# A fused attention and two-layer-block kernel: row sums on VectorE in the first softmaxes, another order of sums in a weight pair, and alternating first token tiles

## The chip, the cores and the metric

The kernel runs on one core of a Trainium2 chip. The metric is device time in microseconds (us) of one execution. TensorE (PE) multiplies matrices into PSUM banks, ScalarE (ACT) and VectorE (DVE) read PSUM and SBUF, GpSimd (POOL) works on SBUF alone, SyncE (SP) issues all DMA transfers. Each engine works through its own instructions in the order in which they were written down; an instruction that waits holds up everything behind it on its engine.

## What is computed

Three stages follow each other, all in float32 with 2304 tokens of 512 channels:

```
# attention in chunks of 64 tokens, 4 batches x 8 heads, head width 64
scores = q_c @ k_c.T / 8
attn = exp(scores - max(scores)); attn = attn / (sum(attn) + 1e-9)
x = (attn @ v_c) laid out as (2304, 512)
# mixture of 4 experts, F = 1024
p = probs / (probs.sum(-1) + 1e-9)
x = sum over e of p[:, e] * (relu(x @ w1[e]) @ w2[e])
# normalised gated block, F = 1536
xn = x / sqrt(mean(x*x) + 1e-6) * rms_g
g, val = xn @ w_gate, xn @ w_val
out = (g * sigmoid(g) * val) @ w_out
```

## The kernel before, in words

**Number format.** Each float32 operand of a matmul is split into two pieces of a shorter format, a high one (`hh`, `[:, 0]`) and a low one (`hl`, `[:, 1]`), and a product is three matmuls (line 22). The low piece is always one subtraction that waits for the copy that makes the high piece.

**Tokens.** The 18 tiles of 128 tokens go through in three sets of six. A set has two halves of three tiles (index b = 0 or 1, 384 tokens). After attention come the expert stage of all three sets ("moe", eight blocks of work per set) and then the gated stage of all three ("glu", three blocks per set), 33 blocks in all.

**One block** consists of `hidden` for two pairs of hidden columns (in glu for gate and value of each), and then `outer`. `hidden` (line 751) computes four products, for b = 0, 1 and j = 0, 1 (two groups of 128 hidden columns), by seven products of sums of quarters of x and w instead of eight. Each of the seven is six matmuls of 384 columns (`product`, line 701). VectorE combines them: partial sums u2, u3 and five additions per pair, reading PSUM banks named a, b, c and d. A finished combination goes to `use`, which makes hh on ScalarE and leaves the making of hl (and the return of the bank) in a list that `catch_up` empties later. The combinations are finished in the order (1,1), (0,0), (1,0), (0,1).

**`outer`** (line 846) multiplies hh and hl with the second weights for tile t = 0 to 5; tiles 0 to 2 belong to b = 0, tiles 3 to 5 to b = 1. A tile takes 12 matmuls of 512 columns: six of the block's first pair, then six of its second. VectorE adds the result to an accumulator (`flush`). Of its second six, the first tile needs (0,0) and then (0,1) of the pair that `hidden` has only just left.

**Order of the work.** The program is written out in full by Python generators. `Chains.tick`, called after each product and each six matmuls of `outer`, drops a few instructions of side work into the engines' queues: weight splitting (`operands`, ScalarE and GpSimd), decoding of 64-bit weights (VectorE), attention of the next set. `ORDER` (line 27) is the order in which the seven weight parts are made, fetched and summed.

**The start.** Attention of the first six tiles (`attention_unit` with `first_softmax`, line 612) and the first products are interleaved by `Chains.race`, which gives each engine the step that it thinks can begin first, by guessed costs such as `{"ACT": 0.9}`. When TensorE would idle by its guess, `idle` (line 957) fills in transposes into `scratch`. In `first_softmax` the exponentials are eight activations of 128x64 per tile, each with `accum_out`, so that ScalarE gives the row sums. Then VectorE inverts them and GpSimd scales.

Names in the rows: `sc` scores, `e` exponentials, `at` scaled attention, `trA`/`aT` its transpose, `pv` attention times v, `x` split x, `w` a weight or a split weight part, `r` a fetched raw weight, `o` output bank of `outer`.

Of the kernel before, what the change touches and what calls it, by code (L numbers as in the profile page):

```python
# [23 lines left out]

ORDER = (0, 5, 4, 6, 1, 3, 2)


class Slots:  # L30
# [41 lines left out]
class Chains:  # L72
# [6 lines left out]
    def add(self, gen, every=0.0, first=False, busy=None):  # L79

        c = [gen, every, self.clock, every if busy is None else busy]
        self.chains.insert(0, c) if first else self.chains.append(c)
        return c
# [67 lines left out]
def fused_kernel(ctx, tc, qkv, probs, w12, wglu, gvec, out):  # L151
# [460 lines left out]
    def first_softmax(sc, ex, att):  # L612

        mx, nb, rs = (sm.tile([P, 2, HP], F32, tag=f"f{n}", name=n) for n in ("mx", "nb", "rs"))
        for h2 in range(2):
            nc.vector.tensor_reduce(
                mx[:, h2, :].unsqueeze(2), sc[h2][:, :HP * CH].rearrange("p (g n) -> p g n", n=CH), axis=AX.X, op=ALU.max
            )
            yield {"DVE": 0.45 if h2 == 0 else 0.2}, 1
        nc.vector.tensor_scalar(nb, mx, -SCALE, None, op0=ALU.mult)  # L620
        for h2 in range(2):
            yield {"ACT": 0.9}, 1
            for g in range(HP):
                cols = slice(g * CH, (g + 1) * CH)
                nc.scalar.activation(  # L625
                    ex[h2][:, cols], sc[h2][:, cols], AF.Exp, scale=SCALE, bias=nb[:, h2, g:g + 1],
                    accum_out=rs[:, h2, g:g + 1],
                )
            banks.put(sc[h2])
        yield {"DVE": 0.5}, 1  # L630
        nc.vector.tensor_scalar_add(rs, rs, 1e-9)
        nc.vector.reciprocal(rs, rs)
        for h2, e in enumerate(ex):
            yield {"POOL": 0.65}, 1
            nc.gpsimd.tensor_tensor(
                att.rearrange("p (hp r n) -> p hp r n", hp=HP, r=2)[:, :, h2, :],
                e[:, :HP * CH].rearrange("p (g n) -> p g n", n=CH),
                rs[:, h2, :].unsqueeze(2).to_broadcast([P, HP, CH]),
                op=ALU.mult,
            )  # L640
            tp.put(e)
# [74 lines left out]
    def catch_up():  # L716
        while later:
            later.pop(0)()

    def bank(name):  # L720
        if not banks.free():
            work.force(None, banks.free)
        return banks.get(name)
# [27 lines left out]
    def hidden(key, use):  # L751


        w = lambda n: weight((*key, n))
        v = lambda t: t[:, :NB]
        a = bank("a_ps")
        product(a, w(0), 0, True, False)
        p1 = cp.get("p1")
        nc.scalar.copy(p1, v(a))  # L759
        catch_up()  # L760
        b = bank("b_ps")
        product(b, w(5), 5, True, True)
        u2 = cp.get("u2")
        add(nc.vector, u2, v(b), p1)
        banks.put(b)
        cp.put(p1)
        d = bank("d_ps")
        product(d, w(4), 4, True, False)
        c = bank("c_ps")
        product(c, w(6), 6, True, True)  # L770
        u3 = cp.get("u3")
        add(nc.vector, u3, v(c), u2)
        add(nc.vector, v(c), v(d), u3)
        use(1, 1, c)
        product(a, w(1), 1, False, True)
        catch_up()
        use(0, 0, a)
        c = bank("c_ps")
        product(c, w(3), 3, True, True)
        add(nc.vector, v(c), v(c), u3)  # L780
        cp.put(u3)
        catch_up()
        use(1, 0, c)
        product(d, w(2), 2, False, True)
        add(nc.vector, v(d), v(d), u2)
        cp.put(u2)
        catch_up()
        use(0, 1, d)

    hs = {}  # L790

# [54 lines left out]
    def outer(fps, w2, flush, aside):  # L846

        catch_up()
        for t in range(TPS):
            b, r = divmod(t, TPB)  # L850
            ps = bank(f"o_{t}")
            last = (len(fps) - 1, 1, len(PASSES) - 1)
            for k, fp in enumerate(fps):
                for j in range(2):
                    for m, (hx, wi) in enumerate(PASSES):
                        nc.tensor.matmul(  # L856
                            ps, hs[fp, b, j][hx][:, r * P:(r + 1) * P], w2[2 * k + j][:, wi],
                            start=((k, j, m) == (0, 0, 0)), stop=((k, j, m) == last),
                        )
                if k == len(fps) - 1:  # L860
                    flush(t, ps)
                    banks.put(ps)
                work.tick(6 * 0.227)
                aside(t * UF + k)
        for fp in fps:
            for b in range(2):
                for j in range(2):
                    hi, lo = hs.pop((fp, b, j))
                    hh.put(hi)
                    hl.put(lo)  # L870
        w2p.put(*w2)
# [53 lines left out]
    with tc.manual_schedule():  # L925
        units = [[i, i + 1] for i in range(0, NTILE, 2)]
        own = lambda s: units[s * TPS // 2:(s + 1) * TPS // 2]
        make_identity(nc, ident)
        fetching = work.add(fetch())
        lead = [[i] for i in range(TPS)]  # L930
        tiles = [attention_tiles(u) for u in lead]
# [201 lines left out]
```

## Time and profile before

| | us |
|---|---|
| median of 3 runs (1246.80 to 1248.53) | 1246.94 |
| the profiled execution | 1249.17 |
| its span | 1247.4 |
| granted TensorE clock, mean over the span | 0.997 |
| PE busy | 1223.3 (98%) |
| DVE busy | 783.0 (63%) |
| POOL busy | 537.4 (43%) |
| ACT busy | 449.0 (36%) |

The profiled execution lies 1.8 us above its span and 2.2 us above the median of the timed runs. A busy PE is not PE at its peak: matmuls overlap in the record, so time that TensorE loses shows best as the distance between the starts of two matmuls, compared with the usual distance. A clock of 1.00 is 2.4 GHz, 0.50 is 1.2 GHz.

### The profile page before, as it was taken

What the parts mean: (1) busy time and instruction counts of PE and PEld (TensorE: products, weight loads), DVE (VectorE), ACT (ScalarE), POOL (GpSimd) and SP (SyncE); (2) the same over time, 40 slices, a digit from 0 to 9 for tenths busy, and PEclk for the clock granted to TensorE, in tenths of its full rate; (3) what the DMA queues carried; (4) which work ended last, traced back from release to release, by engine and by line L of the source; (5) the groups of instructions that cost most, each with busy time, mean ns of one, the idle gap of its engine ahead of it and who ended that gap; (6) DMA issues with size and microseconds to landing.
All of it is one profiled execution on the core that took longest, in us unless ns stands there. A gap on an engine that the chain in (4) does not pass through costs nothing.

```text
span 1247.4 us, 20675 instructions
## 1 busy us (share of the span) xinstructions
PE 1223.3 (98%) x7253; PEld 1107.0 (89%) x7253; DVE 783.0 (63%) x1388; ACT 449.0 (36%) x1109; POOL 537.4 (43%) x575
## 2 busy tenths in 40 slices
PE   7999999999999999999999999999999999999998
PEld 6888899989997987889999999998998998998997
DVE  3765444456776787677677766786766634763644
ACT  7454333334243233333244224333435341332211
POOL 3696666654463563526355445354313101130100
PEclk9999999999999999999999999999999999999999
DMA  8377455554577697755667677657956935855843
GB/s 293 106 255 284 173 194 186 187 202 157 191 253 250 235 326 262 243 169 207 224 235 269 201 243 252 201 164 259 311 194 233 304 112 197 285 189 186 302 131 124
DMA packets 140215, 274.05 MB, mean 220 GB/s; under 512 B 16208, under 2 KB 16208, under 8 KB 140112
## 3 DMA queue, kind: packets, MB, share of 16 engines
q1 hardware_dynamic: 140112, 272.73, 64.0%
q8 instruction: 58, 0.95, 0.3%
q14 instruction: 45, 0.37, 0.1%
HBM read 210.28 MB, written 62.39 MB: 219 GB/s over the span
## 4 chain that ended last, share of the span: by engine, by line
PE 77%; DVE 8%; POOL 5%; issue 4%; ACT 3%; DMA 2%; SPq 0%; POOLq 0%; DVEq 0%
PE o L856 36%; PE d_ps L706 11%; PE a_ps L706 11%; PE c_ps L706 11%; PE b_ps L706 6%; POOL w L197 3%; DMA w1m<-w 2%; DVE silu L830 2%; POOL tw L197 1%; DVE c_ps L198 1%; PE pv L544 1%; DVE u L198 1%; ACT e L625 1%; PE xT L911 1%; PE sc L497 1%
## 5 line engine op out<-in xcount | busy, mean ns | idle before, releaser
L856 PE MATMUL o<-w,hh 128*128 128x512 f32 x1584 | 492.8, 392 | 5.3 <-ACT hh L796 3.5
L856 PEld LDWEIGHTS o<-w,hh 128*128 128x128 f32 x1584 | 295.7, 188 | 69.4 <-ACT hh L796 5.2
L856 PE MATMUL o<-w,hl 128*128 128x512 f32 x792 | 311.5, 393 | 2.2 <-DVE hl L799 1.2
L197 POOL TENSOR_TENSOR w<-r,w 128x512 fp32r<-128x512 f32 (+1 forms) x146 | 163.4, 1127 | 135.5 <-ACT w L356 76.7
L706 PE MATMUL c_ps<-x,w 128*128 128x384 f32 x1080 | 216.2, 336 | 0.3 <-ACT e L625 0.3
L706 PE MATMUL d_ps<-x,w 128*128 128x384 f32 x984 | 198.6, 336 | 2.4 <-DVE c_ps L198 2.2
L706 PE MATMUL a_ps<-x,w 128*128 128x384 f32 x984 | 198.6, 336 | 0.9 <-ACT p L759 0.9
L706 PEld LDWEIGHTS c_ps<-x,w 128*128 128x128 f32 x1080 | 188.8, 188 | 0.8 <-ACT e L625 0.5
L856 PEld LDWEIGHTS o<-w,hl 128*128 128x128 f32 x792 | 148.9, 188 | 39.2 <-DVE hl L197 4.7
L1049 DVE SCALAR_TENSOR_TENSOR acc<-o,pr,acc 128x512 f32<-128x512 f32 x126 | 94.3, 749 | 135.0 <-PE o L856 134.7
L197 POOL TENSOR_TENSOR hl<-silu,hh 128x384 fp32r<-128x384 f32 x54 | 54.4, 1030 | 288.4 <-ACT hh L833 288.3
L706 PEld LDWEIGHTS a_ps<-x,w 128*128 128x128 f32 x984 | 173.4, 188 | 3.9 <-ACT p L759 1.2
L706 PEld LDWEIGHTS d_ps<-x,w 128*128 128x128 f32 x984 | 172.1, 188 | 4.4 <-DVE c_ps L198 4.3
L198 POOL TENSOR_TENSOR w<-w,sc 128x512 f32<-128x512 f32 x36 | 47.1, 1309 | 163.0 <-DVE sc L415 139.8
L197 POOL TENSOR_TENSOR w<-tw,w 128x256 fp32r<-128x256 f32 x112 | 87.2, 787 | 39.9 <-ACT w L231 34.2
L198 DVE TENSOR_TENSOR u<-b_ps,p 128x384 f32<-128x384 f32 x82 | 45.5, 554 | 88.2 <-PE b_ps L706 46.4
L706 PE MATMUL b_ps<-x,w 128*128 128x384 f32 x492 | 99.0, 335 | 0.0
L759 ACT COPY p<-a_ps 128x384 f32<-128x384 f32 x82 | 39.5, 482 | 162.4 <-PE a_ps L706 162.3
L796 ACT ACTIVATE hh<-c_ps 128x384 fp32r<-128x384 f32 x100 | 49.1, 494 | 131.9 <-DVE c_ps L198 130.3
L198 DVE TENSOR_TENSOR u<-c_ps,u 128x384 f32<-128x384 f32 x82 | 45.6, 556 | 74.1 <-PE c_ps L706 73.5
L231 ACT CAST w<-tw 128x256 fp32r<-128x256 f32 x112 | 42.6, 406 | 136.0 <-POOL tw L197 91.4
L706 PEld LDWEIGHTS b_ps<-x,w 128*128 128x128 f32 x492 | 86.4, 188 | 0.1
(109 smaller groups left out, 1346.5 us busy)
## 6 DMA issues: line engine op xcount, KB each, us to landing
w<-wgv SPq DMA_DIRECT2D x252, 256.0 KB, 3.9
w<-w1m SPq DMA_DIRECT2D x224, 256.0 KB, 5.2
r<-in_w SPq DMA_DIRECT2D x128, 256.0 KB, 4.8
w1m<-w SPq DMA_DIRECT2D x112, 256.0 KB, 2.5
wgv<-w SPq DMA_DIRECT2D x84, 256.0 KB, 4.7
raw<-in_wglu SPq DMA_DIRECT2D x36, 512.0 KB, 3.8
w<-wou SPq DMA_DIRECT2D x36, 512.0 KB, 7.4
wou<-q SPq DMA_DIRECT2D x24, 256.0 KB, 4.4
```

What stands on the lines that cost most here:

```text
L197: sub = lambda eng, o, a, b: eng.tensor_tensor(o, a, b, op=ALU.subtract)
L198: add = lambda eng, o, a, b: eng.tensor_tensor(o, a, b, op=ALU.add)
L231: nc.scalar.copy(halves(out[n])[:, 0], at[part_of[n]])
L497: nc.tensor.matmul(sc[h2][c * CH:(c + 1) * CH, n:n + CH], q, k, start=True, stop=True)
L544: nc.tensor.matmul(ps[n][lo:lo + CH, o:o + CH], vt[a][lo:lo + CH, hp, ch, :], aT[a][lo:lo + CH, q:q + CH], start=True, stop=True,)
L625: nc.scalar.activation(ex[h2][:, cols], sc[h2][:, cols], AF.Exp, scale=SCALE, bias=nb[:, h2, g:g + 1], accum_out=rs[:, h2, g:g + 1],)
L706: nc.tensor.matmul(ps[:, :NB], wv[:, wi, k, :], xs[n][:, xi, k, :], start=(first and k == 0 and m == 0), stop=(last and k == KH - 1 and m ...
L759: nc.scalar.copy(p1, v(a))
L796: nc.scalar.activation(hi, src, AF.Relu)
L830: nc.vector.tensor_tensor(v, ps[:, :NB], v, op=ALU.mult)
L856: nc.tensor.matmul(ps, hs[fp, b, j][hx][:, r * P:(r + 1) * P], w2[2 * k + j][:, wi], start=((k, j, m) == (0, 0, 0)), stop=((k, j, m) == last),
L1049: nc.vector.scalar_tensor_tensor(out=acc[i], in0=ps, scalar=pr[:, i, e:e + 1], in1=acc[i], op0=ALU.mult, op1=ALU.add,)
```

## The change

Four edits. (1) At the start a tiny activation of type Exp on a zeroed column is put ahead of everything. (2) In `first_softmax` the activations lose `accum_out`; two VectorE reductions per tile, one for each half, make the row sums. The costs that `race` is told change, and with them the order of the start. (3) In `hidden` the banks c and d change roles: v4 = d + u2 is made while product 6 runs, then d = c + v4 ends (1,1); bank c goes on accumulating in place of d; the order of finishing is (1,1), (0,0), (0,1), (1,0), and `ORDER` follows. (4) In `outer` the first four groups of six matmuls go tile 0 pair 1, tile 1 pair 1, tile 0 pair 2, tile 1 pair 2, with two output banks open.

```diff
-ORDER = (0, 5, 4, 6, 1, 3, 2)
+ORDER = (0, 5, 4, 6, 1, 2, 3)
...
-                    ex[h2][:, cols], sc[h2][:, cols], AF.Exp, scale=SCALE, bias=nb[:, h2, g:g + 1],
-                    accum_out=rs[:, h2, g:g + 1],
+                    ex[h2][:, cols], sc[h2][:, cols], AF.Exp, scale=SCALE, bias=nb[:, h2, g:g + 1]
                 )
             banks.put(sc[h2])
-        yield {"DVE": 0.5}, 1
+        for h2 in range(2):
+            yield {"DVE": 0.4 if h2 == 0 else 0.8}, 2 - h2
+            nc.vector.tensor_reduce(
+                rs[:, h2, :].unsqueeze(2), ex[h2][:, :HP * CH].rearrange("p (g n) -> p g n", n=CH), axis=AX.X, op=ALU.add
+            )
         nc.vector.tensor_scalar_add(rs, rs, 1e-9)
...
         d = bank("d_ps")
-        product(d, w(4), 4, True, False)
+        product(d, w(4), 4, True, True)
+        v4 = cp.get("v4")
+        add(nc.vector, v4, v(d), u2)
         c = bank("c_ps")
-        product(c, w(6), 6, True, True)
-        u3 = cp.get("u3")
-        add(nc.vector, u3, v(c), u2)
-        add(nc.vector, v(c), v(d), u3)
-        use(1, 1, c)
+        product(c, w(6), 6, True, False)
+        add(nc.vector, v(d), v(c), v4)
+        use(1, 1, d)
         product(a, w(1), 1, False, True)
         catch_up()
         use(0, 0, a)
-        c = bank("c_ps")
-        product(c, w(3), 3, True, True)
-        add(nc.vector, v(c), v(c), u3)
-        cp.put(u3)
+        d = bank("d_ps")
+        product(d, w(2), 2, True, True)
+        add(nc.vector, v(d), v(d), v4)
+        cp.put(v4)
+        catch_up()
+        use(0, 1, d)
+        product(c, w(3), 3, False, True)
+        add(nc.vector, v(c), v(c), u2)
+        cp.put(u2)
         catch_up()
         use(1, 0, c)
-        product(d, w(2), 2, False, True)
-        add(nc.vector, v(d), v(d), u2)
-        cp.put(u2)
-        catch_up()
-        use(0, 1, d)
...
-        for t in range(TPS):
+        last = (len(fps) - 1, 1, len(PASSES) - 1)
+        order = [(t, k) for t in range(TPS) for k in range(len(fps))]
+        order[1], order[2] = order[2], order[1]
+        open_banks = {}
+        for n, (t, k) in enumerate(order):
             b, r = divmod(t, TPB)
-            ps = bank(f"o_{t}")
...
+            if k == 0:
+                open_banks[t] = bank(f"o_{t}")
+            ps = open_banks[t]
...
+        warm = sm.tile([P, 1], F32, tag="warm", name="warm")
+        nc.vector.memset(warm, 0.0)
+        nc.scalar.activation(warm, warm, AF.Exp)
```

ScalarE's queue at the start of the program, before: the exponentials of three tiles stand one behind the other.

```order
L625 ACT_TABLE_LOAD
L625 ACTIVATE e_213,rs<-sc_195,nb 128x64 x4
L625 ACTIVATE e_214,rs<-sc_196,nb 128x64 x4
L625 ACTIVATE e_249,rs<-sc_226,nb 128x64 x4
L625 ACTIVATE e_250,rs<-sc_227,nb 128x64 x4
L625 ACTIVATE e_290,rs<-sc_263,nb 128x64 x4
L526 COPY aT_323<-trA_318 128x512
L625 ACTIVATE e_291,rs<-sc_264,nb 128x64 x4
L315 CAST w_0_360<-r_0_165 128x256
```

The same place now:

```order
L938 ACT_TABLE_LOAD
L938 ACTIVATE warm<-warm 128x1
L625 ACTIVATE e_216<-sc_198,nb 128x64 x4
L625 ACTIVATE e_217<-sc_199,nb 128x64 x4
L315 CAST w_0_289<-r_0_168 128x256
L625 ACTIVATE e_252<-sc_229,nb 128x64 x4
L625 ACTIVATE e_253<-sc_230,nb 128x64 x4
L625 ACTIVATE e_293<-sc_266,nb 128x64 x4
L526 COPY aT_333<-trA_328 128x512
L625 ACTIVATE e_294<-sc_267,nb 128x64 x4
```

The table load stands alone in front, and the split of the first fetched weight (`w_0<-r_0`) has moved from behind the third tile's exponentials to behind the first tile's; on GpSimd the subtraction that belongs to it has moved likewise ahead of the first tile's scaling.

VectorE's queue in the last value pair of the program, before (lines 198: the sums of `hidden`; 830: silu times value; 197: the low piece of (0,1)):

```order
L198 TENSOR_TENSOR u_13685<-b_ps,p_13675 128x384
L198 TENSOR_TENSOR u_13701<-c_ps,u_13685 128x384
L198 TENSOR_TENSOR c_ps<-d_ps,u_13701 128x384
L830 TENSOR_TENSOR silu<-c_ps,silu 128x384
L830 TENSOR_TENSOR silu<-a_ps,silu 128x384
L198 TENSOR_TENSOR c_ps<-c_ps,u_13701 128x384
L830 TENSOR_TENSOR silu<-c_ps,silu 128x384
L198 TENSOR_TENSOR d_ps<-d_ps,u_13685 128x384
L830 TENSOR_TENSOR silu<-d_ps,silu 128x384
L197 TENSOR_TENSOR hl<-silu,hh 128x384
```

The same place now:

```order
L198 TENSOR_TENSOR u_13701<-b_ps,p_13691 128x384
L198 TENSOR_TENSOR v_13710<-d_ps,u_13701 128x384
L198 TENSOR_TENSOR d_ps<-c_ps,v_13710 128x384
L833 TENSOR_TENSOR silu<-d_ps,silu 128x384
L833 TENSOR_TENSOR silu<-a_ps,silu 128x384
L198 TENSOR_TENSOR d_ps<-d_ps,v_13710 128x384
L833 TENSOR_TENSOR silu<-d_ps,silu 128x384
L198 TENSOR_TENSOR c_ps<-c_ps,u_13701 128x384
L197 TENSOR_TENSOR hl<-silu,hh 128x384
L833 TENSOR_TENSOR silu<-c_ps,silu 128x384
```

There are as many additions as before. One of the two that stood behind product 6 (c) now needs product 4 (d) only, and the low piece of (0,1) is no longer the last row but stands ahead of the row for (1,0).

TensorE's queue at the beginning of the last `outer`, before (`o_13745` is tile 0; `w_13605` and `w_13616` are the weights of the first pair, `w_13625` and `w_13639` of the second):

```order
L706 MATMUL d_ps<-x_12472,w_2_13603 128x384 x6
L856 MATMUL o_13745<-w_13605,hh 128x512 x2
L856 MATMUL o_13745<-w_13605,hl 128x512
L856 MATMUL o_13745<-w_13616,hh 128x512 x2
L856 MATMUL o_13745<-w_13616,hl 128x512
L856 MATMUL o_13745<-w_13625,hh 128x512 x2
L856 MATMUL o_13745<-w_13625,hl 128x512
L856 MATMUL o_13745<-w_13639,hh 128x512 x2
L856 MATMUL o_13745<-w_13639,hl 128x512
```

The same place now (`o_13761` is tile 0, `o_13768` tile 1):

```order
L709 MATMUL c_ps<-x_12490,w_3_13619 128x384 x6
L863 MATMUL o_13761<-w_13621,hh 128x512 x2
L863 MATMUL o_13761<-w_13621,hl 128x512
L863 MATMUL o_13761<-w_13632,hh 128x512 x2
L863 MATMUL o_13761<-w_13632,hl 128x512
L863 MATMUL o_13768<-w_13621,hh 128x512 x2
L863 MATMUL o_13768<-w_13621,hl 128x512
L863 MATMUL o_13768<-w_13632,hh 128x512 x2
L863 MATMUL o_13768<-w_13632,hl 128x512
L863 MATMUL o_13761<-w_13643,hh 128x512 x2
L863 MATMUL o_13761<-w_13643,hl 128x512
L863 MATMUL o_13761<-w_13655,hh 128x512 x2
```

Six matmuls of tile 1 have moved in ahead of the first use of the second pair, and the product that ends last is number 3, whose result only tiles 3 to 5 read.

## Rows read from the trace of the kernel before

**Rows 1.** Waits of TensorE's weight loads: what waited, for whom, total us, times, longest.

```profile
PEld o L856 <- ACT hh L796: 5.2, 5, 1.9
PEld o L856 <- DVE hl L197: 4.7, 9, 0.6
PEld d_ps L706 <- DVE c_ps L198: 4.3, 7, 1.4
PEld o L856 <- DVE hl L799: 3.7, 8, 1.2
...
PEld o L856 <- ACT hh L833: 2.8, 9, 0.8
PEld o L856 <- POOL w L197: 1.9, 2, 1.2
PEld trA L521 <- POOL at L604: 1.6, 3, 0.8
```

**Rows 2.** Timeline (start, us, instruction, count), all engines, the start.

```profile
5.94 1.28 ACT L625 ACT_TABLE_LOAD   x1 [5.94 <-DVE nb L620]
...
7.23 0.31 ACT L625 ACTIVATE e<-sc,nb 128x64 f32<-128x64 f32 x1
7.45 0.19 ACT L625 ACTIVATION_READ_ACCUMULATOR e<-sc,nb 128x1 f32 x1
...
8.87 0.33 SPq L471 DMA_DIRECT2D qk_b<-in_qkv  x1
...
10.30 1.18 POOL L635 TENSOR_TENSOR at<-e,rs 128x256 f32<-128x256 f32 x2 [9.00 <-DVE rs L632]
...
13.79 1.93 PE L544 MATMUL pv<-aT,v 64*64 64x64 f32 x32 [0.83 <-ACT aT L526]
...
36.63 10.67 PE L706 MATMUL c_ps<-x,w 128*128 128x384 f32 x60
```

**Rows 3.** Stretches: length, busy us of each engine (instructions), granted clock, DMA.

```profile
13.80:38.70 24.90, 22.90 (x372) 21.01 (x373) 12.87 (x50) 21.15 (x103) 11.66 (x18) 0.93 0.75 244
271.20:275.50 4.30, 3.65 (x22) 3.33 (x20) 4.16 (x7) 0.50 (x1) 2.30 (x2) 1.00 0.60 192
383.00:386.00 3.00, 3.00 (x9) 2.32 (x8) 2.15 (x5) 2.51 (x4) 0.00 (x0) 0.51 1.05 402
```

**Rows 4.** Timeline, TensorE, first tile of the last block.

```profile
1227.93 0.62 PE L856 MATMUL o<-w,hh 128*128 128x512 f32 x2
...
1228.63 0.66 PE L856 MATMUL o<-w,hh 128*128 128x512 f32 x2
1229.44 0.50 PE L856 MATMUL o<-w,hl 128*128 128x512 f32 x1
1229.78 0.62 PE L856 MATMUL o<-w,hh 128*128 128x512 f32 x2
```

**Rows 5.** Timeline, TensorE, the first tile of the block that begins at 377.

```profile
379.25 0.74 PE L856 MATMUL o<-w,hh 128*128 128x512 f32 x2 [0.32 <-ACT hh L796]
380.79 0.50 PE L856 MATMUL o<-w,hl 128*128 128x512 f32 x1 [0.80 <-DVE hl L799]
381.78 0.73 PE L856 MATMUL o<-w,hh 128*128 128x512 f32 x2 [0.49 <-ACT hh L796]
```

**Rows 6.** Timeline, TensorE, the first tile of the block that begins at 481.

```profile
483.58 0.51 PE L856 MATMUL o<-w,hl 128*128 128x512 f32 x1 [0.35 <-DVE hl L799]
485.29 0.73 PE L856 MATMUL o<-w,hh 128*128 128x512 f32 x2 [1.20 <-ACT hh L796]
```

**Rows 7.** Timeline, TensorE, the first tile of the block that begins at 81.

```profile
85.25 0.74 PE L856 MATMUL o<-w,hh 128*128 128x512 f32 x2 [1.47 <-ACT hh L796]
...
87.64 0.55 PE L521 MATMUL trA<-ident,at 128*128 128x128 f32 x3
```

**Rows 8.** Groups by line, VectorE: instruction, count | busy us, mean ns | idle before.

```profile
L198 DVE TENSOR_TENSOR u<-c_ps,u 128x384 f32<-128x384 f32 x82 | 45.6, 556 | 74.1 <-PE c_ps L706 73.5
...
L616 DVE TENSOR_REDUCE mx<-sc 128x4 f32<-128x256 f32 x12 | 4.4, 410 | 8.6 <-PE sc L497 8.6
```

More of the change, by code (lines that the diff above doesn't have):

```diff
@@ L848, in outer @@
         catch_up()
-        for t in range(TPS):
-            b, r = divmod(t, TPB)
-            ps = bank(f"o_{t}")
[L852 to L864, printed above, removed]
+        last = (len(fps) - 1, 1, len(PASSES) - 1)
[3 more added lines that the diff above has]
+        for n, (t, k) in enumerate(order):
+            b, r = divmod(t, TPB)
+            if k == 0:
+                open_banks[t] = bank(f"o_{t}")
+            ps = open_banks[t]
+            for j in range(2):
+                for m, (hx, wi) in enumerate(PASSES):
+                    nc.tensor.matmul(
+                        ps, hs[fps[k], b, j][hx][:, r * P:(r + 1) * P], w2[2 * k + j][:, wi],
+                        start=((k, j, m) == (0, 0, 0)), stop=((k, j, m) == last), skip_group_check=True,
+                    )
+            if k == len(fps) - 1:
+                flush(t, ps)
+                banks.put(ps)
+            work.tick(6 * 0.227)
+            aside(n)
         for fp in fps:
```

## The prediction

> **What bounds the kernel now.** I read the busy shares first: TensorE has work through nearly the whole span, no other engine comes near, so the time is TensorE's work plus what it loses between matmuls. The waits of its weight loads [rows 1] then say where it loses. Four of the rows, 5.2 + 4.7 + 3.7 + 2.8 us, have line 856 waiting for the high or low pieces of the hidden values: the start of `outer`. One (4.3) has the last product of a pair waiting for VectorE to have read bank d. The rest is weights that GpSimd hasn't split (1.9) and attention tiles. A weight load runs ahead of its matmul, so these rows count more than the end is late by; what a place is worth I take from distances of matmul starts. The third thing to read is the start of the program [rows 2], and the stretch from the first `pv` to the first product of the second half [rows 3].
>
> **The change part by part.**
>
> *Starts of `outer`, gated stage.* In the last block the usual distance is 0.70 us for three matmuls (1227.93 to 1228.63), 0.23 each. From 1228.63 to 1229.44 two matmuls take 0.81 instead of 0.46, and the next one 0.34 instead of 0.23 [rows 4]: 0.35 + 0.11 = 0.46 lost. TensorE waits there for the low piece of (0,1), the last thing that `hidden` finishes. The row for hl L197 counts nine such waits, as many as the stage has blocks [rows 1]. Now (0,1) is finished one product earlier (six matmuls; 60 take 10.67 us [rows 2], so 1.0 us) and is needed six matmuls of `outer` later (1.4 us). Its low piece stands behind one addition on VectorE that waits for the last product, and is then late by some 1.5 us of VectorE work against 3.9 us (17 matmuls at 0.23) until TensorE asks for it. What is late next is (1,0), which tile 3 reads after 36 matmuls, 8 us. I take 9 x 0.46 = 4.2; bounds 3 and 5.5 (two of the nine also wait for hh L833).
>
> *Starts of `outer`, expert stage.* Three blocks stand out. At 379: 1.54 instead of 0.46, then 0.99 instead of 0.23, and 0.3 idle before it [rows 5], together 2.2; after these gaps the granted clock is 0.51 over 3 us [rows 3], which costs another 1.5. With 2.4 us more slack only the low piece of (0,1) is still late, by 0.2, and the clock has no gap to fall after: 3.5 gained. At 483: 1.71 instead of 0.23, with 0.35 idle before it [rows 6]: 1.8, of which I leave 0.3 since VectorE has softmax work in its queue: 1.5. At 85.25: 1.47 idle; but 2.4 us further, at 87.64, TensorE transposes an attention tile [rows 7] that GpSimd, by the trA row [rows 1], scales only just in time or too late, so a TensorE that is earlier waits there instead. VectorE's chain to that tile is shorter by the one addition that no longer stands in it (0.56 [rows 8]): gain 0.6. Bounds for the three: 2.5 and 7.
>
> *First block.* The second pair's output weights are late, 1.9 us of waits [rows 1]. Asked for 1.4 us later, they cost about 0.5. But then TensorE enters the next pair earlier than GpSimd's splitting, which has no pause there, and a copy on ScalarE that stands behind a split weight gives some back: 0.7 gained (0 to 1.5).
>
> *Attention transposes.* The row for trA and L604 has 1.6 us in three waits [rows 1]; one addition less in VectorE's chain before them: 0.8 (0 to 1.2).
>
> *The pair's sums.* The wait of product 2 for the addition that read d (4.3 us, seven times [rows 1]) becomes a wait of product 3 for the addition that reads c, at the same place. Five additions remain five. Where VectorE is idle, the reading is done 0.56 earlier [rows 8]; but at the largest of these waits VectorE was busy 4.16 of the 4.30 us before [rows 3], and in a full queue it makes no difference which of the additions comes first. I take 0.4; bounds 0 and 3. The changed `ORDER` only follows the use of the parts. The v4 addition waits for product 4 with side work queued behind it; what hides that is product 6, 1.0 us, during which VectorE has nothing else that TensorE needs.
>
> *The start.* The table load (1.28 us between the first maximum and the first exponential [rows 2]) goes ahead of the first scores and is hidden by their transfer. VectorE takes on two reductions per tile, 0.41 each like those for the maximum [rows 8]; the first lies beside ScalarE's work, the last lengthens each tile's chain by 0.4. None of the 1.28 reaches the first tile's scaling on GpSimd: the split of `w_0` now stands ahead of it. That weight's transfer is over at about 8.87, for the `qk_b` issue at that time is the one eight transfers behind it and waits for it. With a copy of 0.5 and a subtraction like one of the two scalings (1.18 for two), scaling begins near 10.0 instead of 10.30 [rows 2]. The gain comes behind it. The copy aT, for which the first `pv` waited, stands behind twenty exponentials before and now. They began at 7.23; now the first eight are done when `w_0` arrives, and the other twelve follow its copy, from 9.4 on. From an activation's start to its accumulator read is 0.22 us, and the read takes 0.19, part of it beside the next [rows 2]. Without the read I take 0.22 each, so 12.0 for the twelfth and, with the copy, 12.7 for `pv` instead of 13.79: 1.1 gained (0.4 if an activation still takes 0.28). From 13.8 to 38.7 (36.63 plus 12 of the 60 products, 2.1) TensorE was busy 22.9 of 24.9 us at a mean clock of 0.93 [rows 3]: without gaps and at full clock 21.2. That is 34.0 at best, 34.9 with a tile's wait here and there; 1.1 + 2.0 + 1.7 = 4.8 gained at best, 0.4 to 1.1 if the stretch stays as it is. I take 3.3, nearer the best, since both the gaps and the slow clock lie in a stretch whose order has changed.
>
> The Trainium skill ("ScalarE: Activation LUTs", What ACT_TABLE_LOAD costs) says that an activation with a bias column takes 280 ns plus 0.83 ns per element and that neighbours overlap by 93 ns, an estimate of 0.24 us for these; by that the start would gain 0.3 less and the sum be 14.7. The same section adds a drain of 1.38 us to each table load; the row does not show one, the load ends at 7.22 and the first activation starts at 7.23 [rows 2], and by the page the sum would be 16.4.
>
> **Sum.** 4.2 + 3.5 + 1.5 + 0.6 + 0.7 + 0.8 + 0.4 + 3.3 = 15.0. The profiled execution took 1249.17 us, so 1234.2 for it; the timed runs have a median 2.2 lower, 1246.94, so **1232** for the median.
>
> **Rivals.**
>
> *The start gives nothing back (12%).* Transfers arrive when they did, and `race` with its new guesses puts instructions where they block. For: `w_0` stands in front on two engines and takes up what the table load gave. Against: 2.0 us of gaps and a slow clock lie behind that place. Time: 1246.9 - 11.7 = 1235.2; with the start 1 us worse than before, 1236.
>
> *The crowded blocks keep their waits (12%).* The waits at 379 and 483 come from queues on VectorE and ScalarE; shifted by some us, side work falls elsewhere and other blocks get such waits. For: all three stand in stretches with decoding or attention. Against: 2.4 us more slack holds in all 33 blocks. Time: 1246.9 - 9.4 = 1237.5.
>
> *The sums free more than I grant (10%).* If VectorE is late at those seven waits only by the second addition, 3 us of the 4.3 go, and the start reaches its best: 1246.9 - 15.0 - 2.6 - 1.5 = 1227.8.
>
> *Slower: v4 stalls VectorE (4%).* The new addition waits for product 4 in each of 82 pairs, and decoding queued behind it starts later; if VectorE then falls behind, product 3 waits for c at each pair. It decides once a pair costs over 15.0/82 = 0.18 us. At 0.25 us it is 20.5, and 1232 + 20.5 = 1252.5. For: VectorE is full in some stretches [rows 3]. Against: the addition u2 and the side work ahead of v4 take most of product 4's microsecond already, and before, u3 waited for product 6 at the same place.
>
> *It doesn't do what it says (2%)*: the starts of `outer` wait for something else just behind (a bank for tile 1, a weight). Banks are handed out in turn, and the two that `outer` takes first were not the last pair's. Then only the start remains, 1243.
>
> **How the numbers follow.** The likeliest case (60%) lies between 1229 and 1235. With the rivals, 1226 to 1238 leaves out the slower case, the one without effect, and tails of the others, under 2 in 10. Repeated runs of this kernel agree to about 0.2%, so less than 2.5 us counts as no change. Faster by more: all but the slower case and a small part: 0.94. Same 0.02, slower 0.04.
>
> **What would show it.** Right: the four rows of line 856 waiting for hh and hl nearly gone, under 2 us in all; no half-clock stretch near 380; the block of products that began at 36.63 beginning near 33 and the first `outer` near 43.5 instead of 47; the wait of the last product for VectorE still there, now under c_ps, above 2 us. Wrong: that last row gone (the sums were worth more), new waits of PE for GpSimd or ScalarE in the first 100 us (the start is given back), or the gap of [rows 4] still in each gated block.

## The result, and the profile after

The changed kernel takes **1231.45 us** (median of 4 runs, 1231.08 to 1231.62) beside 1246.87 for the kernel before (4 runs, 1246.09 to 1248.53): a ratio of 0.987, 95% interval 0.9855 to 0.9884. Forecast were 1232 and a range of 1226 to 1238. The profiled execution took 1231.08 us, span 1229.3 against 1247.4.

First the busy shares, from the page of the changed kernel: TensorE is busy for 99% of a span that is 18.1 us shorter, and still bounds it.

```profile
PE 1212.4 (99%) x7254; PEld 1106.1 (90%) x7254; DVE 786.6 (64%) x1396; ACT 447.1 (36%) x1062; POOL 543.0 (44%) x580
```

Then the waits of TensorE's weight loads (what waited, for whom, total us, times, longest), which answer to [rows 1].

```profile
PEld pv L544 <- ACT aT L526: 3.7, 7, 1.1
PEld c_ps L709 <- DVE d_ps L198: 3.5, 4, 1.7
PEld trA L521 <- POOL at L604: 2.9, 3, 2.0
PEld a_ps L709 <- ACT p L762: 2.0, 2, 1.2
...
PEld o L863 <- POOL w L197: 1.4, 2, 1.0
```

The four rows of `outer` waiting for hh or hl, 16.4 us in all, have no successor. The wait for the pair's sums is there, now under c_ps. The transposes' wait for a scaled tile has grown (1.6 to 2.9), and a_ps has a second wait for the copy p, at 66.65, in a pair that TensorE now enters earlier. The largest of the transposes' waits stands at the place that was at 87.64 before [rows 7]:

```profile
84.33 0.66 PE L521 MATMUL trA<-ident,at 128*128 128x128 f32 x4 [1.62 <-POOL at L604]
```

The timeline of TensorE in the last block answers to [rows 4]: 0.68 to 0.69 us per three matmuls, without a gap.

```profile
1208.98 0.62 PE L863 MATMUL o<-w,hh 128*128 128x512 f32 x2
1209.44 0.39 PE L863 MATMUL o<-w,hl 128*128 128x512 f32 x1
1209.67 0.61 PE L863 MATMUL o<-w,hh 128*128 128x512 f32 x2
...
1210.35 0.61 PE L863 MATMUL o<-w,hh 128*128 128x512 f32 x2
```

The timeline of the start answers to [rows 2].

```profile
0.73 1.28 ACT L938 ACT_TABLE_LOAD   x1 [0.73 <-PEq L1132]
2.02 0.20 ACT L938 ACTIVATE warm<-warm 128x1 f32<-128x1 f32 x1
...
8.94 0.41 ACT L315 CAST w<-r 128x256 fp32r<-128x256 f32 x1 [1.21 <-DMA r<-in_w]
9.26 2.57 ACT L625 ACTIVATE e<-sc,nb 128x64 f32<-128x64 f32 x12
...
10.11 1.19 POOL L638 TENSOR_TENSOR at<-e,rs 128x256 f32<-128x256 f32 x2
...
12.92 1.15 PE L544 MATMUL pv<-aT,v 64*64 64x64 f32 x32
...
33.88 10.64 PE L709 MATMUL c_ps<-x,w 128*128 128x384 f32 x60
44.36 0.62 PE L863 MATMUL o<-w,hh 128*128 128x512 f32 x2
```

The split of w_0 stands ahead of the first scaling (10.11; forecast near 10.0, before 10.30), `pv` begins at 12.92 (forecast 12.7, before 13.79), the products at 33.88 (before 36.63), the first `outer` at 44.36 (before 47.14). The stretch of [rows 3] from 13.80 to 38.70 has the same busy time, so nearly as much idle time (1.93 us, before 2.00), but full clock:

```profile
13.80:38.70 24.90, 22.97 (x360) 20.73 (x357) 17.75 (x61) 18.56 (x71) 12.29 (x18) 1.00 0.77 259
```

Twelve exponentials take 2.57 us, (2.57 - 0.31) / 11 = 0.21 from one to the next. The Trainium skill ("ScalarE: Activation LUTs", What ACT_TABLE_LOAD costs) has figures from which the estimate was 0.24 and a drain on top of each table load; here the measurement decides: 0.21, and the activation behind the load starts at 2.02 where the load ends at 2.01. (The 0.3 us that the forecast took off by that estimate is 0.2: twelve times 0.02.)

One loss is new. In the block before 373.82 TensorE waits 1.39 (1.56 by the distance of starts) for the addition that reads c; before it was 0.28. The timeline shows why for 1.0 of it: a 128x6 step of the norm stands ahead of that addition on VectorE and took 1.17 us, until an instruction of GpSimd had ended (370.86 + 1.27 = 372.13; 370.97 + 1.17 = 372.14). The addition begins right behind it. The rest of the wait comes from other work in VectorE's queue.

```profile
370.86 1.27 POOL L197 TENSOR_TENSOR w<-r,w 128x512 fp32r<-128x512 f32 x1 [1.17 <-ACT w L356]
...
370.97 1.17 DVE L898 TENSOR_TENSOR z<-y 128x6 f32<-128x6 f32 x1
372.07 0.55 DVE L198 TENSOR_TENSOR d_ps<-c_ps,v 128x384 f32<-128x384 f32 x1
...
372.67 0.79 PE L709 MATMUL c_ps<-x,w 128*128 128x384 f32 x3 [1.39 <-DVE d_ps L198]
```

In the kernel before the same step fell where GpSimd was idle (its next instruction begins at 375.25):

```profile
374.92 0.17 DVE L891 TENSOR_TENSOR z<-y 128x6 f32<-128x6 f32 x1
```

The Trainium skill ("SBUF — State Buffer", SBUF: two separate sides) says that VectorE, with two inputs from SBUF, and GpSimd take a shared port for a whole instruction, and the later one waits. The two rows agree. So does a pair of instructions that two of the experiments share. In e5, VectorE begins 0.05 us ahead of GpSimd, takes 0.68 us, and GpSimd takes 1.77; in e10, VectorE begins 0.29 us behind, takes 1.55, and GpSimd takes 1.29 (timelines of e5, then of e10).

```profile
341.18 0.68 DVE L411 SCALAR_TENSOR_TENSOR w<-sc,w 128x512 f32<-128x512 uint32 x1
341.23 1.77 POOL L197 TENSOR_TENSOR w<-r,w 128x512 fp32r<-128x512 f32 x1
```

```profile
341.42 1.55 DVE L411 SCALAR_TENSOR_TENSOR w<-sc,w 128x512 f32<-128x512 uint32 x1
341.13 1.29 POOL L197 TENSOR_TENSOR w<-r,w 128x512 fp32r<-128x512 f32 x1
```

In e10 and e11 the addition behind that step comes so late that TensorE waits 1.0 us for it (at 343.50 and 342.36); in e5 and in the changed kernel it does not wait there.

### The profile page after: what moved, and what is told of

The parts are those of the page before. It is cut to its first block, busy times and chain, and to the rows that moved or that the text cites. A ratio compares the mean times of both kernels' runs of the same rounds, so it can differ in the third digit from the quotient of the medians.

```text
span 1229.3 us, 20740 instructions
## 1 busy us (share of the span) xinstructions
PE 1212.4 (99%) x7254; PEld 1106.1 (90%) x7254; DVE 786.6 (64%) x1396; ACT 447.1 (36%) x1062; POOL 543.0 (44%) x580
## 4 chain that ended last, share of the span: by engine, by line
PE 91%; DVE 2%; POOL 2%; issue 2%; ACT 1%; DMA 1%; SPq 0%; POOLq 0%; DVEq 0%; ACTq 0%
PE o L863 42%; PE a_ps L709 13%; PE c_ps L709 13%; PE d_ps L709 13%; PE b_ps L709 7%; PE pv L544 1%; POOL w L197 1%; POOL tw L197 1%; PE xT L918 1%; PE sc L497 0%; DMA r<-in_w 0%; PE trA L521 0%; DVE d_ps L198 0%; DVE s L197 0%; DMA w1m<-w 0%
## 5 line engine op out<-in xcount | busy, mean ns | idle before, releaser
L863 PE MATMUL o<-w,hl 128*128 128x512 f32 x792 | 308.4, 389 | 0.0
L799 ACT ACTIVATE hh<-d_ps 128x384 fp32r<-128x384 f32 x92 | 45.4, 493 | 121.0 <-DVE d_ps L198 121.0
L836 ACT CAST hh<-silu 128x384 fp32r<-128x384 f32 x72 | 35.9, 513 | 103.5 <-DVE silu L833 103.4
```

Source lines behind the costliest of these rows:

```text
L799: nc.scalar.activation(hi, src, AF.Relu)
L836: nc.scalar.copy(hi, v)
L863: nc.tensor.matmul(ps, hs[fps[k], b, j][hx][:, r * P:(r + 1) * P], w2[2 * k + j][:, wi], start=((k, j, m) == (0, 0, 0)), stop=((k, j, m) = ...
```

## The experiments

All medians, with the ratio to the kernel before on the same chip. That kernel's medians there were 1246.84 to 1247.36.

| run | what it is | median us (range) | ratio, 95% interval |
|---|---|---|---|
| e1_order | before + order of `outer` | 1236.63 (1236.53 to 1238.24) | 0.992, 0.9906 to 0.9933 |
| e2_sums | before + pair's sums and `ORDER` | 1237.18 (1237.06 to 1239.97) | 0.9926, 0.9913 to 0.9938 |
| e3_start | before + start | 1244.56 (1242.2 to 1248.17) | 0.9981, 0.9971 to 0.9991 |
| e4_table | before + early table load | 1245.71 (1244.03 to 1247.67) | 0.9992, 0.9983 to 1.0001 |
| e5_nostart | changed - start | 1234.96 (1234.39 to 1235.12) | 0.9901, 0.9888 to 0.9915 |
| e9_finish | changed, sums of before | 1272.92 (1272.62 to 1273.13) | 1.0206, 1.0192 to 1.022 |
| e10_tile | e5 + the added tile, no load | 1233.47 (1233.42 to 1234.46) | 0.9891, 0.9876 to 0.9906 |
| e11_load | e5 + the load, no added tile | 1236.32 (1234.82 to 1237.28) | 0.9915, 0.9897 to 0.9932 |
| e6_six | changed + sixth addition | 1232.67 (1232.52 to 1236.17) | 0.9891, 0.9877 to 0.9904 |
| e7_pcopy | changed + copy p early | 1232.16 (1231.19 to 1234.12) | 0.9882, 0.9868 to 0.9895 |
| e8_both | e6 + e7 | 1232.68 (1231.95 to 1234.78) | 0.9886, 0.9868 to 0.9903 |
| e12_later | changed, transposes later | 1230.27 (1228.95 to 1230.91) | 0.9866, 0.985 to 0.9883 |

To see where a kernel gains I put the starts of its `outer` blocks side by side (us from the start of the span; blocks counted from 0, the gated stage is 24 to 32). A gain is where the distance to the column of before changes.

| | before | e1 | e2 | e4 | e5 | changed |
|---|---|---|---|---|---|---|
| block 0 | 47.14 | 45.65 | 45.58 | 45.35 | 45.61 | 44.36 |
| block 3 | 159.22 | 157.14 | 156.94 | 157.27 | 157.61 | 155.52 |
| block 10 | 377.38 | 375.16 | 375.75 | 375.01 | 376.32 | 373.82 |
| block 11 | 412.52 | 407.38 | 407.76 | 408.55 | 407.27 | 404.72 |
| block 14 | 522.55 | 515.25 | 516.28 | 518.47 | 514.25 | 511.56 |
| block 15 | 556.06 | 548.75 | 549.53 | 551.94 | 547.47 | 544.75 |
| block 19 | 679.85 | 672.54 | 673.32 | 675.51 | 671.26 | 668.33 |
| block 24 | 852.19 | 844.74 | 845.42 | 847.50 | 843.36 | 840.08 |
| last matmul | 1243.17 | 1230.67 | 1231.09 | 1238.05 | 1229.03 | 1225.09 |

**e1_order.**

```diff
+        order = [(t, k) for t in range(TPS) for k in range(len(fps))]
+        order[1], order[2] = order[2], order[1]
```

> The kernel before with only the loop of outer changed (the first product of the second pair for tile 0 and of the first pair for tile 1 change places); hidden and the start stay. Theory: what the starts of outer lost is lateness of the second pair's pieces, and the change of order asks for them six matmuls (1.4 us) later. In the nine gated blocks the lateness at matmuls 9 to 11 is 0.3 to 0.6 us, so all of it goes: 4.8 us. Near 379 the waits at matmuls 6, 8 and 9 add up to 2.2 us; 0.8 stays, and with a smaller gap the clock may or may not fall (1.5). Near 483 2.0 less 1.4, so 0.6 stays. Near 85 nothing, since the transpose behind it waits. First block 0.5. Sum 4.8 + 1.4 + 1.4 + 0.5 = 8.1 to 9.6: 1238.5 (1237 to 1240). Rival A, only the earlier finish of (0,1) in hidden helps: 1246. Rival B, the order alone is enough for every block: 1235.

Measured 1236.63, 2 us less than expected and below the range. From block 24 to the last matmul it gains 12.50 - 7.45 = 5.05 (expected 4.8), in block 10 2.9 (1.5 of it the half clock), in block 13 1.9. The first 1.5 of its column are not its own: its start is that of before, yet the first `outer` begins 1.49 earlier, because the kernel before spent 14 to 18 at a granted clock of 0.59 in its profiled execution and e1 did not (nor did e2, e5 and e10, which have that start too). Stretches of the two (length, busy us of PE, PEld, DVE, ACT, POOL, granted clock, DMA share, GB/s), before and e1:

```profile
14.00:18.00 4.00, 4.00 (x62) 3.72 (x64) 1.59 (x7) 3.20 (x16) 1.86 (x3) 0.59 1.03 376
```

```profile
14.00:18.00 4.00, 4.00 (x109) 3.70 (x106) 2.59 (x10) 4.00 (x19) 2.71 (x5) 1.00 1.03 372
```

**e2_sums.** `hidden` and `ORDER` as in the change, `outer` and the start as before:

```diff
+        product(d, w(2), 2, True, True)
+        add(nc.vector, v(d), v(d), v4)
...
+        use(0, 1, d)
+        product(c, w(3), 3, False, True)
```

> The kernel before with only hidden and ORDER changed: (0,1) finished a product earlier and (1,0) last, the wait moved from bank d to bank c; outer keeps its order. Theory: (0,1) is ready 1.0 us earlier, more than the gated blocks' lateness of 0.3 to 0.6, so these give 4.8 us here too; near 379 the waits at matmuls 6 and 8 are for a_ps, which hidden finishes where it did, so only the 0.8 at matmul 9 goes and the clock still falls; near 483 1.0 of 2.0; the sums' own waits give about 0.4. Sum 4.8 + 0.8 + 1.0 + 0.4 = 7.0: 1240 (1238 to 1242). If both e1 and e2 hold, their gains overlap by about 5 us and may not be added. Rival A: (1,0), now last, is late in its turn and the gated blocks keep their gap, 1246. Rival B: all blocks are freed, 1235.

Measured 1237.18, 2.8 us less than expected and below the range. The gated blocks gain 12.08 - 6.77 = 5.3; block 10 gains 3.1, of which 1.5 is the half clock of the profile before; block 13 0.7. Of the 8.9 us that `outer` waited for hh and hl in the expert stage [rows 1], 4.4 stay, and the wait for the sums goes from 4.3 us to 3.4 (weight loads of e2, total us, times, longest):

```profile
PEld o L856 <- DVE hl L799: 4.4, 6, 1.1
...
PEld c_ps L706 <- DVE d_ps L198: 3.4, 4, 1.7
```

The new wait before block 10 comes from here: e2 loses 1.28 there, e1 nothing.

**e3_start.** `first_softmax` and the three lines of `warm` as in the change, the rest as before.

> The kernel before with only the start changed (table load early, row sums on VectorE); outer and hidden stay. Theory: the first outer begins about 2.8 us earlier, near 44.4, the granted clock is 1.00 from 12 to 24; the first outer waits for the second pair's split weights as before (2.1 us), and up to 0.7 is given back at a copy on ScalarE in the next pairs. 1244.5 (1243.8 to 1245.5). Rival: the weights' splitting on GpSimd does not get earlier with the start, so the first outer waits 2.8 longer for them and nothing is left: 1246.9.

Measured 1244.56, as expected, but with 6 us between its shortest and its longest run, which go with the granted clock: span 1240.4 us at 1.0, 1246.4 at 0.997. In its profiled execution 15 filler transposes ahead of the first tile took 3.46 us, in the changed kernel 1.94 with the same code (timelines of e3 and of the changed kernel): 0.23 us each instead of 0.13. That looks like the lower clock, but the stretch has a granted clock of 1.00 in e3's profile, so the reason is not shown. `outer` then begins at 45.84, not 44.36.

```profile
9.60 3.46 PE L965 MATMUL scratch<-ident 128*128 128x128 f32 x15
```

```profile
9.02 1.94 PE L969 MATMUL scratch<-ident 128*128 128x128 f32 x15
```

**e4_table.** 

```diff
+        warm = sm.tile([P, 1], F32, tag="warm", name="warm")
+        nc.vector.memset(warm, 0.0)
+        nc.scalar.activation(warm, warm, AF.Exp)
```

> The kernel before with only the early table load; ScalarE still writes the row sums with the exponentials. Theory: the split of w_0 stands in front on ScalarE and GpSimd and eats part of the 1.28 us; the twelve exponentials behind it are at 0.28 us each instead of 0.21, so the first pv begins 0.8 to 1.0 later than in the changed kernel (near 13.8 instead of 12.92), and the start gives 0.5 to 1.5 of its 2.8: 1246 (1245.2 to 1246.9). Rival A: the table load is all that the start gave, first outer near 44.4 and 1244.5. Rival B: nothing, or a little worse, 1247.2, because w_0 now comes before the first scaling.

The size is as expected (1.15 us, the interval touches none), the reason is not: `pv` begins at 12.58, earlier than in the changed kernel, and the first `outer` at 45.35, only 0.25 ahead of e1 and e2 with the start of before. Something else gives the rest (e10, e11). e4 shows one more thing. It has the waits of [rows 5], within 0.04 us, and its clock did not fall behind them: e4 first, then the stretch of before at the same place.

```profile
376.90 0.73 PE L856 MATMUL o<-w,hh 128*128 128x512 f32 x2 [0.36 <-ACT hh L796]
378.44 0.50 PE L856 MATMUL o<-w,hl 128*128 128x512 f32 x1 [0.81 <-DVE hl L799]
379.44 0.74 PE L856 MATMUL o<-w,hh 128*128 128x512 f32 x2 [0.49 <-ACT hh L796]
```

```profile
380.00:385.00 5.00, 5.00 (x23) 4.13 (x23) 4.42 (x9) 2.57 (x4) 0.00 (x0) 1.00 1.02 384
```

```profile
382.00:387.00 5.00, 5.00 (x15) 3.77 (x15) 3.11 (x7) 2.56 (x4) 0.00 (x0) 0.66 1.05 395
```

The block is 1.58 us shorter in e4 for that alone. e3, with the same waits as e4, has the half clock again (0.70 from 380 to 384). So the same gap can be followed by a half clock or not, and an edit that removes the gap cannot be credited with it from one profile. Each kernel was profiled once, so how often it falls in one kernel is not shown.

**e5_nostart.** `hidden`, `ORDER` and `outer` of the change, `first_softmax` and the start of before.

> The changed kernel with the start of before (table load at the first exponential, row sums by ScalarE): both edits of the starts of outer and nothing else. Theory: the start alone gave 2.3 in e3, and of that some is a clock that fell or not; the first outer begins near 45.6, 1.2 later than in the changed kernel: 1233.5 (1232.5 to 1234.5). e1 and e2 together are then worth 13.4 where their sum is 19.9: 6.5 is counted twice, 5.0 of it in the gated blocks, which either edit frees alone, and the rest near 379. Rival A, the start is worth what the prediction gave it (3.3 or more): 1235. Rival B, the gains of e1 and e2 add up further and the start gives nothing: 1231.5. Beside it: the blocks of before, e1 and e2 are 0.05 us longer than those of the kernels with the early table load (outer 16.13 instead of 16.11); if the early load makes that, it is 16.13 here.

Measured 1234.96: rival A. The two edits are worth 1246.87 - 1234.96 = 11.9 together (12.4 against the kernel before on e5's chip, 1247.36) and 10.2 and 9.7 apart, so 7.5 to 8.0 is gained by either; the start, with the added tile, is worth 3.5 here. But of these only 1.25 stand at the first `outer` and 0.8 more by block 3. From there to the end e5 falls behind the changed kernel evenly, 1.8 us in 30 blocks.

**e9_finish.** The changed kernel with the additions of before, (0,1) finished first:

```diff
-        product(d, w(4), 4, True, True)
-        v4 = cp.get("v4")
-        add(nc.vector, v4, v(d), u2)
+        product(d, w(4), 4, True, False)
...
+        add(nc.vector, u3, v(c), u2)
+        add(nc.vector, v(c), v(d), u3)
...
+        product(d, w(2), 2, False, True)
```

> The changed kernel with the sums of before (u3 for two values, d accumulated), but finished in the changed order: (0,1) by product 2 before (1,0) by product 3. Product 2 now asks for bank d one product earlier than in before, behind two additions that wait for product 6. Theory: two additions take 0.47 + 0.56 and a release some 0.05 behind the end of product 6, and product 1 covers 1.04, so each of 82 pairs waits 0.05 to 0.2, and the seven waits of before (3.2 by starts) grow by up to 1.0 each: 1231.5 + 4 to 16 + 5, 1244 (1238 to 1252). The new arrangement of the sums is what makes the new finishing order free. Rival: the arrangement of the sums is worth nothing and the finishing order alone does it: 1231.5.

Measured 1272.92: 41.5 us slower than the changed kernel and 26 slower than before. The direction is the theory's, the size three times as large: the wait stands in 76 pairs (weight loads of e9, then TensorE and VectorE at one ordinary pair of the expert stage).

```profile
PEld d_ps L709 <- DVE c_ps L198: 49.6, 76, 2.5
```

```profile
611.79 1.20 PE L709 MATMUL c_ps<-x,w 128*128 128x384 f32 x6
612.83 1.21 PE L709 MATMUL a_ps<-x,w 128*128 128x384 f32 x6
614.24 0.97 PE L709 MATMUL d_ps<-x,w 128*128 128x384 f32 x4 [0.21 <-DVE c_ps L198]
...
613.03 0.56 DVE L198 TENSOR_TENSOR u<-c_ps,u 128x384 f32<-128x384 f32 x1 [1.45 <-PE c_ps L709]
613.62 0.57 DVE L198 TENSOR_TENSOR c_ps<-d_ps,u 128x384 f32<-128x384 f32 x1
```

Products run 1.04 apart, so d_ps was due at 613.87; it begins at 614.24, and its second matmul is 0.11 late too: 0.48 per pair, times 82 is 39. What I left out is that the last matmul of product 6 starts 0.17 before product 1 and takes 0.34; the addition starts 0.20 after product 1 has begun. Here one product does not cover two additions; in the kernel before, where two products stand between, only five pairs lost time. So the new order of finishing needs the new sums.

**e10_tile and e11_load.** e5 with one or the other half of the early activation:

```diff
+        warm = sm.tile([P, 1], F32, tag="warm", name="warm")
+        nc.vector.memset(warm, 0.0)
```

```diff
+        warm = psm[:, 0, :]
+        nc.vector.memset(warm, 0.0)
+        nc.scalar.activation(warm, warm, AF.Exp)
```

> The kernel of e5 (start of before) with the one-column tile of the early activation and its memset on VectorE, but no early activation. The tile shifts every later buffer, operands of matmuls among them, by 192 bytes. In e5 a block from one start of outer to the next is 0.055 us longer than in the changed kernel, with single matmuls of 231 to 236 ns at each start of outer where 227 is usual; over the program that is 1.9 us. Theory A, the buffers' place makes that: outer 16.11, few such matmuls, and 1233.1. Theory B, the early load itself makes it: outer 16.13 as in e5, and 1235.0.

> The kernel of e5 (start of before) with the early activation done in a buffer that is there already, so that no buffer moves: the early table load alone, row sums by ScalarE. Theory A, the buffers' place makes the shorter blocks: outer 16.13 as in e5; the start gains what e4 did at the first outer (0.2), 1234.7. Theory B, the early load makes them: outer 16.11 and 1232.9.

Theory A in both. From block 15 to block 19 it is 123.57 us in e10 and 123.79 in e11, as the first matmuls of the two blocks show (timelines of e10, then of e11):

```profile
548.17 0.62 PE L860 MATMUL o<-w,hh 128*128 128x512 f32 x2
...
671.74 0.62 PE L860 MATMUL o<-w,hh 128*128 128x512 f32 x2
```

```profile
547.28 0.63 PE L860 MATMUL o<-w,hh 128*128 128x512 f32 x2
...
671.07 0.63 PE L860 MATMUL o<-w,hh 128*128 128x512 f32 x2
```

Before, e1, e2 and e5 have 123.79 too; e3, e4, e6, e7, e8, e12 and the changed kernel have 123.57 or 123.58: all that have the tile, none that has not (e9 has it too, but its waits hide it). Beside the changed kernel, e10 is 3.42 us behind at block 15 and 3.41 at block 19, while e5 goes from 2.72 to 2.93 and to 3.94 at the end: the even drift of e5 is the tile's. By medians the tile is worth 1.5 us, though the intervals of e5 and e10 overlap, and the load nothing: e11 is 1.4 above e5, with its clock at 0.997 to 0.999. In its trace e11 is 1.2 ahead of e5 at block 2 (120.85, e5 122.07) and loses 1.0 of that in the wait at 342.36.

**e6_six, e7_pcopy, e8_both**, on the changed kernel, look for what is left at the waits for c and for p.

```diff
+        u3 = cp.get("u3")
+        add(nc.vector, u3, v(c), u2)
...
+        c = bank("c_ps")
+        product(c, w(3), 3, True, True)
+        add(nc.vector, v(c), v(c), u3)
```

```diff
+        if then:
+            then()
         work.tick(6 * 0.1735, busy=True)
...
+        product(a, w(0), 0, True, False, lambda: nc.scalar.copy(p1, v(a)))
```

> The changed kernel with a sixth addition per pair (c + u2 is kept in SBUF), so that product 3 opens a bank of its own and TensorE waits for no addition of its pair. Theory: the waits of c_ps for VectorE (1.56, 1.0, 0.24) go, 2.8 us; 82 additions of 0.47 more lie on VectorE, where it is idle for most of the span, but near 370, 480 and 535 it is full and the pieces come later; 1229.5 (1228 to 1232). Rival: in the full stretches the extra addition makes waits elsewhere (hl or hh at the starts of outer, trA) that cost more than they free: 1233 or more.

> The changed kernel with the copy of the first product (p) issued to ScalarE right behind the product, ahead of the side work that stands before it now. Theory: at 66.65 and 541.53 product 1's bank waits for that copy, which stands behind a cast of weights: 0.64 + 0.11 and 1.08 + 0.11 go, 1.9 in all: 1229.6 (1229 to 1230.5). Rival: a cast that must wait for the product's end behind the copy makes weights late, and the time stays: 1231.5.

> The sixth addition of e6 and the early copy of e7 together, on the changed kernel. In e6 the waits of product 3 went, but those for the copy p grew (0.64, 0.36 and 2.42 at 542.93); in e7 the copy's waits went at 66.65 and halved at 543.49, but a wait of product 3 grew (2.35). Theory: each edit met the other's wait behind the one that it freed, and together both are gone: from 1232.7 of e6 less 0.7, 0.4 and about 1.4 at those three places, 1230 (1229 to 1231.2). Rival: a queue that is full gives its lateness to whoever is next (hl at the start of outer, trA), and the time stays between 1231.3 and 1233.

None is faster, as the rivals had it; that one is slower is not shown either, since the intervals overlap with that of the changed kernel. In e6 the waits for c are gone and TensorE waits for p and hl (e6, then e7):

```profile
PE a_ps L709 <- ACT p L762: 2.9, 3, 2.3
...
PE o L868 <- DVE hl L807: 0.8, 1, 0.8
```

```profile
PE c_ps L709 <- DVE d_ps L198: 3.0, 2, 2.2
...
PE a_ps L709 <- ACT p L763: 0.4, 1, 0.4
```

In e7 the wait for c near 373 is 2.35 instead of 1.56, and the clock falls behind it. e8 keeps 1.9 at 542.60 for p and has 1.04 and 1.08 at the start of block 10. In these three runs the lateness of a full queue went to whoever asked next.

**e12_later.**

```diff
-        yield from work.pause(2.5)
+        yield from work.pause(4.5)
...
-        yield from work.pause(1)
+        yield from work.pause(2.5)
```

> The changed kernel with an attention tile's transposes issued 2 us later behind its scores, and its pv 1.5 us later behind its transposes. Theory: in the block at 78.46 TensorE, now earlier, waits 1.78 for the transposes' scaled tile (84.33) and 1.18 for the copy aT (90.81), and 0.45 at 503.20; these go: 1231.5 less 3.4, 1228.1 (1227 to 1229.5). Rival: the later transposes fall where their bank or the following unit is waited for, or the last unit is forced at the end of its set, and the waits only move: 1231 to 1233.

Measured 1230.27, 1.2 below the changed kernel and between the ranges of theory and rival; the intervals of the two ratios overlap, so that it is faster is not shown. The three waits went and 5.8 us were gained by block 15. Then 2.18 came back in one wait of c_ps for VectorE, with the clock at half behind it, and about 1.5 more at 909 and 930 (stretches of e12):

```profile
786.00:790.00 4.00, 1.99 (x12) 1.67 (x11) 4.00 (x8) 0.16 (x1) 1.51 (x1) 1.00 0.86 271
790.00:794.00 4.00, 4.00 (x14) 3.32 (x15) 3.63 (x8) 2.85 (x7) 0.00 (x0) 0.65 0.32 95
```

## Why the prediction was right, and where it was not

The total was right by medians: 15.4 us gained, 15.0 forecast. The profiled execution came to 1231.08 where the sum said 1234.2: it gained 18.1. By its steps, against the profiled executions:

| term | forecast | measured |
|---|---|---|
| starts of `outer`, gated | 4.2 (3 to 5.5) | 5.1, two blocks of 0.7 to 0.8 and seven of 0.5 |
| block at 379 | 3.5 | 4.2, of which about 1.5 clock |
| block at 483 | 1.5 | 2.3 |
| block at 85 | 0.6 | -0.1 |
| first block | 0.7 | 1.0, less 0.7 given back at 66.65: 0.3 |
| transposes | 0.8 (0 to 1.2) | 0.5 |
| pair's sums | 0.4 (0 to 3) | 0.4: five waits of 3.16 became three of 2.80 |
| start | 3.3 (0.4 to 4.8) | 2.8, of which 1.5 the clock of one execution |
| place of the buffers | not seen | 1.7 |
| sum | 15.0 | 17.2 of the 18.1; the rest lies in places of 0.2 or less |

*Starts of `outer`.* The mechanism was right and a little under-sized in the gated blocks: the two that also waited for hh give 0.7 and 0.8. The remark that the transpose would take over at 85 was right and not severe enough: the wait at 84.33 is 1.78, and the gain of 0.6 is a loss of 0.1.

*Block at 379.* "the clock has no gap to fall after: 3.5 gained" took 1.5 from a half clock that e4 does not have behind the same waits. It is shown for the profiled execution only.

*The start* is the step that failed in kind. "the gaps and the slow clock lie in a stretch whose order has changed" assigned 1.7 us of clock to the change; e1, e2 and e5 have the old start and full clock there. Of the 2.8 us at the first `outer`, `pv` brought 0.9 (forecast 1.1) and the clock 1.5; 0.4 is left for the gaps, of which the forecast had up to 2.0. What the start itself gives by medians is 1233.47 - 1231.45 = 2.0 (e10 to the changed kernel); e5's trace says the same, 2.1 by block 3. Put into the kernel before it gives less: e3 gained 2.3 by medians, with a spread of 6 us, and some 1.5 of that is the tile. So e3 met its forecast in good part for another reason than the one given. The early load alone gives nothing that I could show. The median came out right by luck: a gain of 1.5 that no step had, the shift of the buffers by the new tile, filled the place of the clock. The medians allot 11.9 to `outer` and the sums (forecast 11.7 of the 15.0), 1.5 to the shift and 2.0 to the start, each to about 1 us.

*The pair's sums.* Right in size, and the rival that v4 stalls VectorE did not come. What the step did not say is what e9 shows: the new arrangement gains little over before, and without it the new order of finishing would cost 41.5.

*What was to show it.* The rows of hh and hl are gone, no half clock stands near 380, the wait for the sums is there at 3.5. The first `outer` came at 44.36 instead of 43.5. The warning sign, new waits for GpSimd and ScalarE in the first 100 us, came too (84.33, 66.65, 90.81), and cost what the first blocks then lack.

## What to carry to other kernels

Lateness of half a microsecond that recurs in each block can be removed by asking later or by finishing earlier, and the two don't add: 10.2 and 9.7 made about 12. Two additions that free an accumulator needed two products behind them here; one was too few. Do not credit an edit with a half-clock stretch of one profile; look whether a second kernel with the same code has it.

## What the hardware showed that I had not expected

A tile that shifts all later buffers (by 192 bytes in the layout; the traces hold no addresses) changed TensorE's time by 0.05 us per block of 31 us: at the start of an `outer` in e11 (block 17) six of eight matmul distances are 231 to 236 ns where 227 is usual, in e10 three are 230 to 232. Thirteen profiles, five without the tile and eight with it, agree, and e11 rules out the table load and the memset. That it is the place of the operands is the reading that is left; why the place matters was not tried.

The granted clock fell to half behind gaps in some executions and not in others with the same gaps (before, e3 and e4 near 380; near 86 it fell in e10 and not in e5, each behind an idle time of 1.95 us), and at the start without an edit there.

A 128x6 instruction of VectorE took 1.17 us beside GpSimd and 0.17 without it. Which of the two engines waits was decided by which began first (0.05 us in e5). Where such a step stands ahead of an addition that TensorE needs, TensorE waits up to that microsecond longer.
